# Two of four small tiled matmul groups moved to places where the TensorE tile shape changes anyway

## The chip, the cores and the metric

The kernel runs on one core of one Trainium2 (trn2) chip. The metric is the device time of one execution in microseconds (us). Times are medians of several executions. Each kernel also has one execution recorded by the hardware profiler; times inside it are counted from the first instruction. All runs told here are of the fast state, but for one single run (e8) whose state is unknown; the granted TensorE clock was 0.999 or 1.000 in all profiles.

## The reference, cut to what matters

Two attention blocks work on the same 2048 tokens (D = 1024, 32 heads of 32), and a gate mixes them. The change concerns block A, a linear attention:

```python
pq, pk = phi(q), phi(k)
kv  = einsum("bhsd,bhse->bhde", pk, v)      # one 32x32 matrix per head
num = einsum("bhqd,bhde->bhqe", pq, kv)
o   = num / (einsum("bhqd,bhd->bhq", pq, z)[..., None] + 1e-6)
a   = o.reshape(B, S, D) @ wo
...
return g * a + (1 - g) * b
```

The kernel never forms `num`. It multiplies each head's 32x32 `kv` into the 32 rows of `wo` that belong to the head, which gives a new weight "W2", and later applies W2 to the normalized `pq`. Making W2 is 64 small matmuls (32 rows, 32 columns of the array, 512 columns streamed), in four groups of 16, called events.

## The kernel before: the parts that matter

The kernel has eight banks of PSUM, the memory in which its matmuls accumulate. Four belong to `ps_pj`, the projection banks, a ring of buffers that every large matmul group uses. Four belong to `ps_1`, which exists only in the first stages; the score tile `s2b` and the output tile `po` of the next stage take over its banks.

```python
for g in range(2):                                    # KV, 128x64 tiles
    kvp = ps_1.tile([P, 4, 64], F32, name="kv_ps", tag="p1")
    for c in range(4):
        for kt in range(KT):
            for j in range(2): ...                    # 64 matmuls of 64 columns
    nc.vector.tensor_copy(out=KVT[:, 4 * g:4 * g + 4, :], in_=kvp[:])
# [...]
def w2_event(g, half):                                # 16 matmuls, 32x32 tiles
    def go():
        w2p = [ps_1.tile([P, 512], F32, name="w2_ps", tag="p1") for _ in range(4)]
        for j in range(4):
            for r in range(4):
                rs = slice(32 * r, 32 * r + 32)
                nc.tensor.matmul(w2p[r][32 * j:32 * j + 32, :],
                                 lhsT=KVT[rs, 4 * g + j, (r % 2) * 32:(r % 2) * 32 + 32],
                                 rhs=WoA[half][rs, 4 * g + j, :], start=True, stop=True)
        for r in range(4):
            (nc.scalar.copy if r % 2 else nc.vector.tensor_copy)(
                out=WoA[half][:, 4 * g + r, :], in_=w2p[r][:])
    return go
# [...]
units = [u for t in range(4) for u in v_units(t)]     # V projection, 128x128 tiles
interleave(units, [(8 + 12 * (2 * g + half), w2_event(g, half)) for g in range(2) for half in range(2)])
for t in range(12):                                   # the query stage
    for u in v_units(4 + t): u()
    for u in qa_units(t, bank1, qa_finish): u()       # qa_finish: phi, then normalize on VectorE
# [...]
nc.vector.memset(po[:], 1.0)                          # po lies in banks that ps_1 gave back
# [...] then the quads: K and Q of block B in 64x64 tiles, four slots of 8 steps each
```

TensorE's order is the program's, and VectorE's is too inside the first and the later stages. The memset of `po` stands between these, and the scheduler of the kernel language puts it into VectorE's order where its model thinks fit. A quad fills four banks, in four slots (the prediction counts them from one: its "second slot" is slot 1). Slots 0 and 1 each add the first half of the sums of two banks, a tiny read ("seen") separates them from slots 2 and 3, and then ScalarE and VectorE copy the banks out as `kt` and `qz`.

The softmax here doesn't subtract the row's maximum and nothing guards it: scores larger than these inputs give would overflow.

## Time and profile before

| what | before |
|---|---|
| time, median of 3 | 473.01 us (472.91 to 473.46) |
| span in the profile | 471.7 us |
| TensorE busy | 467.6 us, 99% |
| chain of waits: TensorE's share | 98% |
| four W2 events | about 1.9 us (worked out below; the printed chain counts 4 x 0.36 = 1.4 us) |

In the views PE stands for TensorE's matmuls, PEld for its weight loads, DVE for VectorE, ACT for ScalarE, POOL for GpSimd and SP for SyncE, which issues the DMA transfers; a "q" behind a name is that engine's sequencer. The page of the kernel before: the span, the busy line (engine, busy us, share of the span, instructions) and the chain that ended last, by engine.

```profile
span 471.7 us, 13176 instructions
...
PE 467.6 (99%) x5765; PEld 251.1 (53%) x5765; DVE 278.4 (59%) x602; ACT 168.7 (36%) x272; POOL 15.3 (3%) x30
...
PE 98%; DMA 1%; DVE 0%; issue 0%; DVEq 0%
```

TensorE is almost never idle and holds 98% of the chain, so in the main only TensorE's own time, or a wait of TensorE, can change the total. Here is TensorE in the V stage (timeline view; columns: start us, us, engine and line, operation, out<-in, shapes, count; in brackets the idle time before it and what ended it, "issue" where the profile shows nothing that did).

```profile
116.27 2.21 PE L240 MATMUL kv_ps<-G,WvA 128*64 128x64 bf16 x128
118.41 1.90 PE L295 MATMUL p_ps<-WvB,xT 128*128 128x512 bf16 x8
120.24 0.43 PE L283 MATMUL w_ps<-WoA,KVT 32*32 32x512 bf16 x16
120.61 2.76 PE L295 MATMUL p_ps<-WvB,xT 128*128 128x512 bf16 x12
123.30 0.43 PE L283 MATMUL w_ps<-WoA,KVT 32*32 32x512 bf16 x16
123.67 2.76 PE L295 MATMUL p_ps<-WvB,xT 128*128 128x512 bf16 x12
```

Two V groups of 12 matmuls start at 120.61 and 123.67, so 3.06 us pass for 12 full matmuls and one event. Full matmuls start 216 ns apart; 12 of them are 2.59 us, and the event costs 0.47 us. Its `busy` of 0.43 us is no measure of that, because matmuls overlap at both ends. The starts of single matmuls show what the 0.47 us is made of:

| step between two starts | ns |
|---|---|
| full matmul to full matmul | 216 |
| last full matmul to first W2 matmul | 309 |
| first to last of the 16 W2 matmuls | 50 |
| last W2 matmul to first full matmul | 318 |
| first full matmul to the second | 226 |

So 309 + 50 + 318 + 226 - 2 x 216 = 471 ns. A W2 matmul streams as many columns as a full one (216 ns), so 93 and 102 ns of the two changes of the tile shape are no streaming. The Trainium skill says in "TensorEngine Tiling (Array Packing)", Key Properties, that changing the tiling mode drains the TensorE. The trace fits that and gives the price, but it does not show that the drain is all of it: between full matmuls a weight load starts 214 ns before its own matmul, at the two changes only 1 and 4 ns before (the two loads take 88 and 96 ns), so a weight load that is no longer hidden is a rival. The 50 ns for 16 starts agree too with "TensorE: Matmul & The Clock Gate", Part 3, which counts about 4 ns per further tile; here it is 3.3.

Last, the border between the query stage (128x128 tiles) and the quads (64x64 tiles), in the timeline of the kernel before.

```profile
217.09 1.92 PE L388 MATMUL q_ps<-xT,WkB 64*64 64x512 bf16 x32
...
218.29 0.69 DVE L157 SCALAR_TENSOR_TENSOR tmp<-p_ps,e 128x512 bf16<-128x512 f32 x1
218.63 0.11 PEld L388 LDWEIGHTS <-WqB 64*64 64x64 bf16 x2
218.84 2.11 PE L388 MATMUL q_ps<-xT,WqB 64*64 64x512 bf16 x32
...
219.04 1.43 PEld L388 LDWEIGHTS <-WqB 64*64 64x64 bf16 x30 [0.30 <-issue]
```

Slot 1 of the first quad (the group of 218.84) fills two banks; one is the bank of the last query group, which VectorE's last phi (218.29 + 0.69 = 218.98) still reads. The slot's matmuls other than the first cannot start before 219.04, 0.19 us late: that is the break between the two weight-load lines. The view names no releaser for it ("issue"); in e6 below, where the same wait is longer, it names this phi. The engine's matmul lines show no gap here, because a matmul is recorded for longer (376 to 400 ns) than the 216 ns to the next one in its tile.

### The profile page before, as it was taken

The numbers are of one execution on the slowest core, as the hardware profiler recorded it, in microseconds if no ns is written. First come the engines' busy times: TensorE is split into PE (matmuls) and PEld (weight loads), VectorE is DVE, ScalarE is ACT, GpSimd is POOL, SyncE is SP. The second block draws the span as 40 slices with busy tenths as digits, with TensorE's granted clock in tenths as the row PEclk, the third lists the DMA queues.
The fourth block names the chain that finished last, engine by engine and source line by source line (L and its number), as shares of the span: only waits on it lengthen the run. The fifth ranks groups of instructions, "written<-read, shape, count | busy, mean of one in ns | idle before, by whom it ended". The sixth has DMA issues, their size and how long they took to land.

```text
span 471.7 us, 13176 instructions
## 1 busy us (share of the span) xinstructions
PE 467.6 (99%) x5765; PEld 251.1 (53%) x5765; DVE 278.4 (59%) x602; ACT 168.7 (36%) x272; POOL 15.3 (3%) x30
## 2 busy tenths in 40 slices
PE   8999999999999999999999999999999999999997
PEld 5444444445444444445677777777764444444444
DVE  0586689990329999999567676767670049800000
ACT  1343321112443333333555555555551134221121
POOL 3300000500000000000000000000000000000000
PEclk9999999999999999999999999999999999999999
DMA  8999970000643233627326364632563913221101
GB/s 220 193 246 374 348 248 0 0 1 1 213 134 108 92 142 128 156 96 248 103 56 100 71 91 96 91 93 63 93 173 67 227 64 79 69 54 45 35 33 46
DMA packets 98732, 55.40 MB, mean 117 GB/s; under 512 B 70130, under 2 KB 90610, under 8 KB 98674
## 3 DMA queue, kind: packets, MB, share of 16 engines
q1 hardware_dynamic: 93378, 49.87, 41.1%
q10 hardware_dynamic: 5296, 4.69, 2.9%
q8 instruction: 45, 0.74, 0.7%
q14 instruction: 13, 0.11, 0.1%
HBM read 26.10 MB, written 15.86 MB: 89 GB/s over the span
## 4 chain that ended last, share of the span: by engine, by line
PE 98%; DMA 1%; DVE 0%; issue 0%; DVEq 0%
PE q_ps L388 27%; PE d_ps L592 12%; PE p_ps L295 12%; PE pk_ps L169 12%; PE g_ps L220 12%; PE e_ps L592 12%; PE p_ps L331 9%; PE po L467 2%; PE s2b L445 2%; DMA xT<-in_A_x_dram 1%; PE kv_ps L240 0%; PE w_ps L283 0%; DVE osb L599 0%; DVEq L599 0%
## 5 line engine op out<-in xcount | busy, mean ns | idle before, releaser
L388 PE MATMUL q_ps<-xT,WqB 64*64 64x512 bf16 x1024 | 69.7, 377 | 0.0
L388 PE MATMUL q_ps<-xT,WkB 64*64 64x512 bf16 x1024 | 69.0, 376 | 0.0
L156 DVE TENSOR_SCALAR e<-e 128x512 f32<-128x512 f32 x64 | 27.1, 423 | 64.0 <-ACT e L155 64.0
L295 PE MATMUL p_ps<-WvB,xT 128*128 128x512 bf16 x256 | 57.9, 379 | 0.0
L169 PE MATMUL pk_ps<-WkA,xT 128*128 128x512 bf16 x256 | 55.7, 380 | 0.4 <-DMA xT<-in_A_x_dram 0.4
L220 PE MATMUL g_ps<-pk,xrow 128*128 128x512 bf16 x256 | 55.4, 379 | 0.0
L450 ACT ACTIVATE PT<-s2b 128x928 bf16<-128x928 f32 (+4 forms) x40 | 34.1, 854 | 45.5 <-PE s2b L445 45.5
L452 DVE TENSOR_TENSOR PT<-PT,mask 128x928 bf16<-128x928 bf16 (+4 forms) x40 | 23.6, 589 | 36.2 <-ACT PT L450 36.2
L331 PE MATMUL p_ps<-WqA,xT 128*128 128x512 bf16 x192 | 43.4, 379 | 0.0
L592 PEld LDWEIGHTS <-pqT 128*128 128x128 bf16 x272 | 26.0, 98 | 29.8 <-issue 0.4
L592 PEld LDWEIGHTS <-OBT 128*128 128x128 bf16 x272 | 26.0, 98 | 29.4
L169 PEld LDWEIGHTS <-xT 128*128 128x128 bf16 x256 | 25.0, 98 | 30.9 <-DMA xT<-in_A_x_dram 0.7
L220 PEld LDWEIGHTS <-xrow 128*128 128x128 bf16 x256 | 25.0, 98 | 30.2
L295 PEld LDWEIGHTS <-xT 128*128 128x128 bf16 x256 | 24.6, 98 | 30.0 <-issue 0.9
L388 PEld LDWEIGHTS <-WkB 64*64 64x64 bf16 x1024 | 34.0, 107 | 11.6 <-issue 0.4
L388 PEld LDWEIGHTS <-WqB 64*64 64x64 bf16 x1024 | 32.5, 107 | 11.1 <-issue 1.0
L599 DVE TENSOR_SCALAR osb<-e_ps,omg 128x128 bf16<-128x128 f32 x1 | 0.4, 351 | 57.6 <-PE e_ps L592 57.6
L155 ACT ACTIVATE e<-pk_ps 128x512 f32<-128x512 f32 x32 | 18.9, 597 | 40.5 <-PE pk_ps L169 36.3
L300 ACT CAST tmp<-p_ps 128x512 bf16<-128x512 f32 x32 | 18.7, 589 | 37.1 <-PE p_ps L295 32.3
L592 PE MATMUL d_ps<-WoA,pqT 128*128 128x512 bf16 (+1 forms) x136 | 30.9, 370 | 0.0
L331 PEld LDWEIGHTS <-xT 128*128 128x128 bf16 x192 | 18.8, 98 | 22.6
L592 PE MATMUL d_ps<-WoB,OBT 128*128 128x512 bf16 (+1 forms) x136 | 30.8, 370 | 0.0
(63 smaller groups left out, 530.3 us busy)
## 6 DMA issues: line engine op xcount, KB each, us to landing
vd<-tmp SPq DMA_DIRECT2D x16, 264.0 KB
xrow<-in_A_x_dram SPq DMA_DIRECT2D x4, 1024.0 KB
out_dram<-osb ACTq DMA_DIRECT2D x31, 128.0 KB
pqd<-tmp SPq DMA_DIRECT2D x12, 256.0 KB
WvA<-in_A_wqkv_dram SPq DMA_DIRECT2D x2, 1024.0 KB
WoA<-in_A_wo_dram SPq DMA_DIRECT2D x2, 1024.0 KB
WvB<-in_B_wqkv_dram SPq DMA_DIRECT2D x2, 1024.0 KB
WqA<-in_A_wqkv_dram SPq DMA_DIRECT2D x2, 1024.0 KB
```

The costliest lines, as they stand in the source:

```text
L155: nc.scalar.activation(out=e[:], in_=pj[:], func=ACT.Exp)
L156: nc.vector.tensor_scalar(out=e[:], in0=e[:], scalar1=1.0, scalar2=1e-6, op0=ALU.min, op1=ALU.add)
L169: nc.tensor.matmul(pj[:], lhsT=xT[:, kt, t * P:(t + 1) * P], rhs=WkA[half][:, kt, :], start=(kt == 0), stop=(kt == KT - 1))
L220: nc.tensor.matmul(pj[:], lhsT=xrow[:, t, kt * P:(kt + 1) * P], rhs=pk[:, t, half * 512:(half + 1) * 512], start=(t == 0), stop=(t == NB - 1))
L295: nc.tensor.matmul(st["pj"][:], lhsT=xT[:, kt, t * P:(t + 1) * P], rhs=WvB[half][:, kt, :], start=(kt == 0), stop=(kt == KT - 1))
L300: nc.scalar.copy(out=v[:, half * 16:(half + 1) * 16, 0:Dh], in_=st["pj"][:].rearrange("p (h e) -> p h e", h=16))
L331: nc.tensor.matmul(st["pj"][:], lhsT=xT[:, kt, t * P:(t + 1) * P], rhs=WqA[half][:, kt, :], start=(kt == 0), stop=(kt == KT - 1))
L388: nc.tensor.matmul(banks[o][64 * j:64 * j + 64, :], lhsT=lhsT(r, kt, j), rhs=rhs(r, kt), start=first and kt == 0, stop=kt == KT - 1, skip_ ...
L445: nc.tensor.matmul(s2b[64 * par:64 * par + 64, pair, :, o:o + w], lhsT=kts[c][r, par, k0:k0 + 64], rhs=qz[r, :, par, q0 % 512:q0 % 512 + w ...
L450: nc.scalar.activation(out=pt[:, :, 0:W_], in_=s2b[:].rearrange("p a b s -> p (a b) s")[:, :, 0:W_], func=ACT.Exp, scale=SCALE)
L452: nc.vector.tensor_tensor(out=pt[:, :, 0:W_], in0=pt[:, :, 0:W_], in1=mask[:, None, base:base + W_].broadcast_to([P, 4, W_]), op=ALU.mult)
L592: nc.tensor.matmul(st["ps"][:, 0:n], lhsT=lhsT, rhs=W[c0 // 512][:, c, c0 % 512:c0 % 512 + n], start=(side == 0 and c == 0), stop=(side == ...
```

## The change

Events should stand where the tile shape changes anyway. The first goes right behind KV (128x64 tiles to 128x128), the last to the end of the query stage (128x128 to 64x64). KV moves to the projection banks, so that the early event finds its own four free. At the end of the query stage VectorE is busy, so ScalarE alone empties the last event's banks. The whole diff:

```diff
--- before.py
+++ after.py
@@ -232,14 +232,14 @@
 
 
             for g in range(2):
-                kvp = ps_1.tile([P, 4, 64], F32, name="kv_ps", tag="p1")
+                kvp = ps_pj.tile([P, 512], F32, name="kv_ps", tag="pj")[:, 0:256].rearrange("p (c d) -> p c d", c=4)
                 for c in range(4):
                     for kt in range(KT):
                         for j in range(2):
                             cols = slice(c * P + 64 * j, c * P + 64 * j + 64)
                             nc.tensor.matmul(kvp[64 * j:64 * j + 64, c, :], lhsT=WvA[g][:, kt, cols],
                                              rhs=G[g][:, kt, cols], start=(kt == 0), stop=(kt == KT - 1))
-                nc.vector.tensor_copy(out=KVT[:, 4 * g:4 * g + 4, :], in_=kvp[:])
+                nc.vector.tensor_copy(out=KVT[:, 4 * g:4 * g + 4, :], in_=kvp)
             WkB = load_w("WkB", B_wqkv, D, "wb")
 
 
@@ -274,7 +274,7 @@
 
 
 
-            def w2_event(g, half):
+            def w2_event(g, half, engines=(nc.vector.tensor_copy, nc.scalar.copy)):
                 def go():
                     w2p = [ps_1.tile([P, 512], F32, name="w2_ps", tag="p1") for _ in range(4)]
                     for j in range(4):
@@ -284,8 +284,7 @@
                                              lhsT=KVT[rs, 4 * g + j, (r % 2) * 32:(r % 2) * 32 + 32],
                                              rhs=WoA[half][rs, 4 * g + j, :], start=True, stop=True)
                     for r in range(4):
-                        (nc.scalar.copy if r % 2 else nc.vector.tensor_copy)(
-                            out=WoA[half][:, 4 * g + r, :], in_=w2p[r][:])
+                        engines[r % len(engines)](out=WoA[half][:, 4 * g + r, :], in_=w2p[r][:])
                 return go
 
             def v_units(t):
@@ -345,12 +344,14 @@
                     nc.sync.dma_start(out=pqd[t * P:(t + 1) * P, :], in_=pn)
 
             units = [u for t in range(4) for u in v_units(t)]
-            interleave(units, [(8 + 12 * (2 * g + half), w2_event(g, half)) for g in range(2) for half in range(2)])
+            w2_event(0, 0)()
+            interleave(units, [(20, w2_event(0, 1)), (40, w2_event(1, 0))])
             for t in range(12):
                 for u in v_units(4 + t):
                     u()
                 for u in qa_units(t, bank1, qa_finish):
                     u()
+            w2_event(1, 1, (nc.scalar.copy,))()
             WqB = load_w("WqB", B_wqkv, 0, "wc")
```

## The prediction

> **What bounds the kernel now.** TensorE does: busy 467.6 of 471.7 us (the page's busy table), and the chain of waits is TensorE for 98% of the span. Only TensorE time on that chain counts. The four W2 events are 1.4 us of it, so all that can be won is small.
>
> **What one event costs** (single instructions of the trace, 119.9 to 123.9 us). A full 128x128 matmul starts 216 ns after the one before it. Where the array goes from 128x128 to 32x32 tiles the step is 309 ns. The 16 W2 matmuls then start within 50 ns, the first full matmul follows 318 ns after the last of them, and the next one is 10 ns late. So one event between full matmuls costs 309+50+318+10-216 = 471 ns; four of them 1.88 us. About 95 to 105 ns of each switch is not streaming. The Trainium skill, TensorEngine Tiling (Array Packing), Key Properties, says that changing the tiling mode drains the TensorE; the trace agrees: from the last KV matmul (128x64 tiles, 16 ns apart) to the first full one takes 128 ns, and from full tiles to the 64x64 tiles of the next stage 309 ns.
>
> **What the change does.** No matmul and no byte is added or removed. Each of the two moved events comes to stand where the tile shape changes anyway, so one switch less is paid: KV to W2 (est. 128 ns), 50, W2 to full 318 replaces KV to full 128. The event costs 368 ns instead of 471: 103 ns saved. At the end, full to W2 309, 50, W2 to 64x64 318 replaces 309: again 368, 103 ns saved. Together about 0.2 us, all on the critical path. KV in the projection banks only frees the four W2 banks for the early event; KV's first copy on VectorE ends at 117.93 us and the KV matmuls at 118.3, so the event should not wait. WoA landed at 57 us.
>
> **A second gain.** In the first quad of the 64x64 stage the second slot's WqB matmul waits from 218.85 to 219.04 us for the bank that VectorE's last phi frees at 218.996 us; three of the four tiles lose 0.19 us. In the new order VectorE's work moves forward with the query matmuls by 0.57 us (0.10+0.47), the stage itself by only 0.21, so this wait should vanish: 0.19 us.
>
> **What could be given back.** ScalarE copies four W2 banks (0.54 us each, back to back) from about 217.2 to 219.4, then does the two "seen" reads that the third slot waits for (its start about 220.2): about 0.4 us of slack, no stall. The memset of po (0.91 us, VectorE, now at 131.6 us in an idle moment) has to wait for the last event's banks, so it moves into or behind the last normalization, shortly before the first qz evictions. VectorE's normalization should end near 223.1, with the memset 224.1; qz becomes ready about 224.0 to 224.15. Roughly zero slack. If the memset is placed before the normalization instead, VectorE waits for ScalarE and TensorE stalls up to 0.9 us at the second quad's second slot (there is a 0.3 us wait already, at 226.07).
>
> **Prediction.** 473.01 - 0.10 - 0.10 - 0.19 = 472.6 us; 80% range 472.2 to 473.3. Faster by over 2%: 0.002; within 2%: 0.996; slower: 0.002.
>
> **Right if the trace shows:** no wait at KV to W2 and a step near 128 ns; two W2 events left between full matmuls at 471 ns; the 64x64 stage starting about 0.2 us earlier; no 0.19 us wait in its second slot; ScalarE's "seen" reads before the third slot.
>
> **Wrong if:** a switch costs differently by tile shape, the scheduler places the memset badly, or ScalarE's copies hold up the seen reads.

## The result, and the profile after

The changed kernel took 472.58 us (472.48 to 472.95, 5 runs) against 473.22 us (472.91 to 473.46, 5 runs) of the kernel before. The ratio is 0.999, with a 95% interval of 0.9976 to 1.0003; it holds 1, so by whole times alone the gain is not shown. A ratio here is the mean time of one kernel's runs over that of the other's of the same rounds, so it is not quite the ratio of the medians. The forecast was 472.6 us.

A part of this difference has nothing to do with the change, so the two profiles have to be compared piece by piece. The last KV matmul starts at 118.284 us before and at 118.105 after, although both programs are the same up to there but for the banks of KV, and KV itself takes 2.019 us from its first start to its last in both: the first stage waits for the transfer of x, and over 14 profiles this start lay between 117.80 and 118.37 us, once at 120.54. From here on I therefore count from the last KV matmul ("late query matmuls" are those of the last four row blocks, which run in 64x64 tiles behind the quads' K and Q):

| us | before | before, profiled again (e8) | after | after again (e11) |
|---|---|---|---|---|
| last KV matmul to first V matmul | 0.128 | 0.128 | 0.494 | 0.493 |
| last KV matmul to first quad matmul | 98.810 | 98.810 | 98.598 | 98.597 |
| first quad matmul to first score matmul | 9.625 | 9.624 | 9.420 | 9.420 |
| from there to the late query matmuls | 116.075 | 115.847 | 115.863 | 115.852 |
| last KV matmul to the end | 353.378 | 353.152 | 352.744 | 352.740 |

Apart from stray pauses (under e8), two executions of one program agree to about 0.01 us in these rows. That is far finer than the whole time, which scatters by some tenths. The page after has these lines in the same places.

```profile
span 470.8 us, 13145 instructions
...
PE 465.1 (99%) x5735; PEld 249.2 (53%) x5765; DVE 277.2 (59%) x600; ACT 169.7 (36%) x274; POOL 15.3 (3%) x30
...
PE 85%; SPq 11%; DMA 2%; DVE 1%; issue 1%; ACT 0%; DVEq 0%
```

Neither the lower busy time nor the chain's 85% means that TensorE works less. The profile holds 5735 matmuls instead of 5765, while both kernels have 5765 weight loads, so some records are missing. At one such hole, the second V matmul after the first event, the printed chain breaks ("issue"), and on the page it runs off to the load of `WvB`, whose two transfers had landed by 61.4 and 64.4 us, over 54 us earlier.

TensorE after the change, in the timeline:

```profile
116.09 2.21 PE L240 MATMUL kv_ps<-G,WvA 128*64 128x64 bf16 x128
118.23 0.43 PE L283 MATMUL w_ps<-WoA,KVT 32*32 32x512 bf16 x16
118.60 4.49 PE L294 MATMUL p_ps<-WvB,xT 128*128 128x512 bf16 x19
123.02 0.43 PE L283 MATMUL w_ps<-WoA,KVT 32*32 32x512 bf16 x16
123.39 4.49 PE L294 MATMUL p_ps<-WvB,xT 128*128 128x512 bf16 x19
```

The event follows KV at once (126 ns after the last KV matmul, as KV to V took 128 ns before), and the first V matmul comes 318 ns after the last of W2. At the border to the quads the steps are 310, 50 and 315 ns where 309 ns stood before. Two events are left between full matmuls, with 20 of these in between (one record is missing in each of the two groups of 19). And the border to the quads:

```profile
216.34 0.43 PE L283 MATMUL w_ps<-WoA,KVT 32*32 32x512 bf16 x16
...
216.70 1.92 PE L389 MATMUL q_ps<-xT,WkB 64*64 64x512 bf16 x32
216.94 2.05 ACT L287 CAST WoA<-w_ps 128x512 bf16<-128x512 f32 x4
...
217.53 0.69 DVE L157 SCALAR_TENSOR_TENSOR tmp<-p_ps,e 128x512 bf16<-128x512 f32 x1
...
218.24 1.63 PEld L389 LDWEIGHTS <-WqB 64*64 64x64 bf16 x32
...
218.45 1.90 PE L389 MATMUL q_ps<-xT,WqB 64*64 64x512 bf16 x32
218.83 0.41 ACT L401 COPY seen<-q_ps 128x1 f32<-128x1 f32 x2
...
220.18 1.90 PE L389 MATMUL q_ps<-xT,WkB 64*64 64x512 bf16 x32
...
220.95 0.91 DVE L373 MEMSET po<- 128x1024 f32 x1 [0.21 <-ACT seen L401]
...
223.96 1.41 DVE L428 TENSOR_SCALAR qz<-q_ps,qsel 128x512 bf16<-128x512 f32 x2
...
225.48 0.84 PE L389 MATMUL q_ps<-xT,WqB 64*64 64x512 bf16 x12
```

Three things are to be seen. VectorE's last phi is over at 218.23 and slot 1 starts at 218.45 with all its tiles: its 32 weight loads are one unbroken group now. ScalarE's four copies (216.94, 2.05 us) and the "seen" reads (218.83) are over at 219.24, 0.9 us before slot 2 (220.18) needs them. The memset of `po` sits inside VectorE's last normalization (220.95, after 0.21 us of idling), and the qz copies follow the normalization without a gap at 223.96. Slot 1 of the second quad waits for them about 0.3 us (225.48), as it did before.

### The profile page after: what moved, and what is told of

It reads as the page before. It is cut to its first block, busy times and chain, and to the rows that moved or that the text cites. A ratio compares the mean times of both kernels' runs of the same rounds, so it can differ in the third digit from the quotient of the medians.

```text
span 470.8 us, 13145 instructions
## 1 busy us (share of the span) xinstructions
PE 465.1 (99%) x5735; PEld 249.2 (53%) x5765; DVE 277.2 (59%) x600; ACT 169.7 (36%) x274; POOL 15.3 (3%) x30
## 4 chain that ended last, share of the span: by engine, by line
PE 85%; SPq 11%; DMA 2%; DVE 1%; issue 1%; ACT 0%; DVEq 0%
PE q_ps L389 27%; PE d_ps L593 12%; PE e_ps L593 11%; PE g_ps L220 11%; PE p_ps L294 11%; PE p_ps L330 8%; SPq L115 4%; SPq L81 4%; DMA WvB<-in_B_wqkv_dram 2%; PE po L468 2%; PE s2b L446 2%; SPq L94 1%; SPq L119 1%; SPq L98 1%; SPq L89 1%
## 5 line engine op out<-in xcount | busy, mean ns | idle before, releaser
L389 PEld LDWEIGHTS <-WkB 64*64 64x64 bf16 x1024 | 32.6, 107 | 12.4 <-DMA vd<-tmp 0.2
```

Of the source, the lines that this page charges most:

```text
L389: nc.tensor.matmul(banks[o][64 * j:64 * j + 64, :], lhsT=lhsT(r, kt, j), rhs=rhs(r, kt), start=first and kt == 0, stop=kt == KT - 1, skip_ ...
```

## The experiments

All twelve gave correct results. "Span" is the time from the last KV matmul to the end in the profile; the kernel before has 353.15 (e8), the changed kernel 352.74. The last column has the kernel before.

| run | median us (runs) | ratio to before, 95% interval | span us | before, median us |
|---|---|---|---|---|
| e1 first event only | 472.97 (5) | 0.9994, 0.9982 to 1.0006 | 353.06 | 473.19 |
| e2 last event only | 472.78 (5) | 0.9992, 0.998 to 1.0004 | 352.91 | 473.19 |
| e3 KV in the old banks | 473.48 (6) | 1.0012, 0.9999 to 1.0026 | 353.32 | 473.19 |
| e4 both engines empty the last event | 473.92 (5) | 1.0016, 1.0003 to 1.0029 | 354.04 | 473.19 |
| e8 before again | 472.97 (1) | none | 353.15 | 472.88 |
| e5 memset twice | 473.47 (4) | 1.0011, 0.9997 to 1.0024 | 353.70 | 472.88 |
| e6 last event 16 matmuls earlier | 473.36 (5) | 1.0006, 0.9992 to 1.0019 | 353.62 | 472.88 |
| e7 an event in front of the output stage | 472.55 (5) | 0.9993, 0.998 to 1.0005 | 352.69 | 472.88 |
| e9 as e6, memset later | 472.78 (4) | 0.9994, 0.998 to 1.0007 | 353.04 | 472.94 |
| e10 the change, memset later | 472.48 (4) | 0.999, 0.9977 to 1.0004 | 352.75 | 472.94 |
| e11 the change again | 472.91 (5) | 0.9998, 0.9985 to 1.0012 | 352.74 | 472.94 |
| e12 e7 again | 472.50 (5) | 0.9988, 0.9975 to 1.0 | 352.69 | 472.94 |

My theory has two parts: a switch of the tile shape saved per moved event (0.10 us each), and a bank wait that vanishes because VectorE's work moves forward more than the quads do (0.19 us). The rivals put the gain on one of the events alone, on the banks, or on ScalarE's doing the copies.

### e1 and e2: each event alone

```diff
 # e1, against the changed kernel
-interleave(units, [(20, w2_event(0, 1)), (40, w2_event(1, 0))])
+interleave(units, [(20, w2_event(0, 1)), (32, w2_event(1, 0)), (44, w2_event(1, 1))])
-w2_event(1, 1, (nc.scalar.copy,))()
 # e2, against the changed kernel; KV goes back to ps_1
-w2_event(0, 0)()
-interleave(units, [(20, w2_event(0, 1)), (40, w2_event(1, 0))])
+interleave(units, [(8, w2_event(0, 0)), (20, w2_event(0, 1)), (40, w2_event(1, 0))])
```

> Only the first W2 event is moved (right behind KV, KV in the projection banks); the other three stay between full matmuls at 20, 32 and 44. Theory (a saved switch of the tiling, and, apart from it, a saved bank wait that belongs to the last event): from the last KV matmul to the first V matmul 0.49 us instead of 0.13, one event of 0.47 us less in the V stage, so the 64x64 stage starts 0.10 us earlier counted from the last KV matmul; the 0.19 us wait at the second slot of the first quad stays. About 0.10 us below before. Rival (both gains come from the early event): the wait goes too, 0.30 us below before.

> Only the last event is moved to the end of the query stage (ScalarE alone empties it); KV keeps its old banks and the first three events stay at 8, 20 and 40. Theory: the 64x64 stage starts 0.10 us earlier counted from the last KV matmul and the 0.19 us wait at the second slot of the first quad is gone; 0.30 us below before, 0.10 above the whole change. Rival (gain needs the early event): the wait stays, 0.10 us below before.

| us | before | e1 | e2 | both |
|---|---|---|---|---|
| last KV matmul to first quad matmul | 98.810 | 98.703 | 98.703 | 98.598 |
| first quad matmul to first score matmul | 9.624 | 9.625 | 9.420 | 9.420 |

Each event saves 0.106 us in front of the quads, and the savings add up. The bank wait stays in e1 (slot 1 of the first quad is late from 218.64 to 218.84) and is gone in e2. So the second gain belongs to the last event alone. The times, 0.22 and 0.41 us below before, have the right order, but their intervals hold 1. In the span e1 gains 0.096 us and e2 0.242 us, which is 0.07 us less than the change's 0.408 us together: 0.06 us of that is a pause of e2 among the late query matmuls (15.383 us from there to the output stage, 15.32 to 15.33 in e1 and in both kernels), whose cause I did not trace.

### e3: KV's banks

```diff
-kvp = ps_pj.tile([P, 512], F32, name="kv_ps", tag="pj")[:, 0:256].rearrange("p (c d) -> p c d", c=4)
+kvp = ps_1.tile([P, 4, 64], F32, name="kv_ps", tag="p1")
```

> The whole change, but KV back in the banks of the W2 events. Theory: the fourth matmul of the early event needs the bank from which VectorE copies KV's second half until about 118.77 us, so TensorE waits from 118.24 to about 118.81 us: 0.55 us lost, and the time ends near 473.1, above before's by what is not covered. Rival (the banks do not matter, the copy is done in time): no wait, time as of the whole change, 472.6.

The timeline of e3 behind KV (this profile began 2.3 us late, in the first stage):

```profile
120.66 0.39 PE L283 MATMUL w_ps<-WoA,KVT 32*32 32x512 bf16 x3
...
120.78 0.42 DVE L242 CAST KVT<-kv_ps 128x256 bf16<-128x256 f32 x1 [0.59 <-PE kv_ps L240]
121.25 0.43 PE L283 MATMUL w_ps<-WoA,KVT 32*32 32x512 bf16 x13 [0.20 <-DVE KVT L242]
...
121.61 0.82 PE L294 MATMUL p_ps<-WvB,xT 128*128 128x512 bf16 x3
```

Three W2 matmuls run, then TensorE waits for VectorE's copy of KV (to 121.20) and goes on at 121.25. From the last KV matmul to V it takes 1.077 us instead of 0.494, so 0.58 us are lost, 0.55 expected. That is more than the whole change gains: in the span e3 is 0.17 us slower than the kernel before. No run moves KV alone, but e1 leaves nothing for it to have saved: its 0.107 us in front of the quads is the one switch. Without the move the early event costs more than it brings.

### e4, e5, e10: how much room VectorE has behind the query stage

```diff
 # e4
-w2_event(1, 1, (nc.scalar.copy,))()
+w2_event(1, 1)()
 # e5
 nc.vector.memset(po[:], 1.0)
+nc.vector.memset(po[:], 1.0)
 # e10: the memset not here, but in the quads' list of events
-nc.vector.memset(po[:], 1.0)
+events.insert(0, (32, lambda: nc.vector.memset(po[:], 1.0)))
```

> The whole change, but the last event's four banks are shared by VectorE and ScalarE as the others are. VectorE's order is the program's, so its two copies (1.3 us) and then the memset of po come behind the last normalization and before the first qz evictions. Theory (VectorE has no slack there): qz starts about 1.25 us later and the second slot of the second quad with it: 1.2 us above the whole change, 473.8. Rival (VectorE's lag is absorbed by the buffers behind it): within 0.2 us of the whole change.

> The whole change with the memset of po done twice on VectorE (0.91 us more in front of the first qz evictions). Theory (no slack left): the qz evictions start 0.9 us later and so does the second slot of the second quad; 0.9 us above the whole change, 473.5. Rival (VectorE still has room): within 0.2 us of the whole change.

> The whole change with the memset of po behind the first qz evictions, out of VectorE's last normalization. Theory (the memset uses up VectorE's slack but no more than that): qz starts at the same time, because it waits for TensorE's last matmul of the quad; span from the last KV matmul 352.74 us as in the whole change, within 0.05. Rival (the memset holds qz up): the 0.33 us wait at the second slot of the second quad shrinks.

The timeline of e4, VectorE's copies of the last event, the memset, the qz copies and slot 1 of the second quad:

```profile
222.79 1.28 DVE L287 CAST WoA<-w_ps 128x512 bf16<-128x512 f32 x2
...
224.43 0.91 DVE L373 MEMSET po<- 128x1024 f32 x1 [0.36 <-DVE WoA L287]
...
225.25 1.32 DVE L428 TENSOR_SCALAR qz<-q_ps,qsel 128x512 bf16<-128x512 f32 x2
...
226.70 0.84 PE L389 MATMUL q_ps<-xT,WqB 64*64 64x512 bf16 x12 [1.24 <-ACT qz L426]
```

VectorE's copies come behind its normalization and push the memset and qz back. TensorE idles 1.24 us before slot 1 of the second quad (226.70), until ScalarE's qz copy, which takes turns with VectorE's on the same banks, is done. From the first quad matmul to the first score matmul e4 takes 10.71 us instead of 9.42, 1.29 us more; in time it is the only run whose interval lies wholly above 1. e5 takes 10.25, 0.83 us more. A further 0.13 us of e5 is a stray pause near 244 us, of the kind described under e8.

In e10 VectorE has the memset behind qz:

```profile
221.47 1.29 DVE L320 TENSOR_TENSOR tmp<-tmp,den 128x512 bf16<-128x512 bf16 x2
...
223.77 1.41 DVE L427 TENSOR_SCALAR qz<-q_ps,qsel 128x512 bf16<-128x512 f32 x2 [1.01 <-PE q_ps L388]
...
225.39 0.91 DVE L511 MEMSET po<- 128x1024 f32 x1 [0.21 <-issue]
```

Now the normalization ends at 222.76 at the latest, VectorE idles 1.01 us before qz, for TensorE, and nothing gets faster (9.421 us). In the changed kernel VectorE idles 0.019 us between the normalization and qz. So it uses up VectorE's room of 1.0 us to the last 0.02 us, and no more. The rival of e4, that buffers absorb the lag, falls.

### e6 and e9: the same event 16 matmuls earlier

```diff
-for u in qa_units(t, bank1, qa_finish):
+for i, u in enumerate(qa_units(t, bank1, qa_finish)):
+    if t == 11 and i == 0:
+        w2_event(1, 1, (nc.scalar.copy,))()
     u()
-w2_event(1, 1, (nc.scalar.copy,))()
 # e9: in addition the memset as in e10
```

> The whole change, but the last event (ScalarE alone) stands 16 full matmuls before the end of the query stage instead of at the border to the 64x64 tiles. Theory: it costs 0.47 us there instead of 0.37, and since the delay now comes before VectorE's last phi, that phi no longer gets ahead of TensorE: the wait of 0.1 to 0.2 us at the second slot of the first quad comes back. 0.2 to 0.3 us above the whole change. Rival (the gain comes from ScalarE alone emptying the banks, or from the event's lateness): as fast as the whole change.

In e6 the stage before the quads took 98.703 us, 0.105 us more than with the event at the border, as expected. But slot 1 of the first quad waited 0.76 us, not 0.1 to 0.2: my expectation missed. The timeline shows why.

```profile
216.24 0.91 DVE L374 MEMSET po<- 128x1024 f32 x1 [0.21 <-ACT e L155]
...
218.57 0.69 DVE L157 SCALAR_TENSOR_TENSOR tmp<-p_ps,e 128x512 bf16<-128x512 f32 x1
...
219.31 1.06 PE L390 MATMUL q_ps<-xT,WqB 64*64 64x512 bf16 x16 [0.39 <-DVE tmp L157]
```

The scheduler had put the memset of `po` in front of VectorE's last two phis, so the last phi ended 0.57 us later than in the kernel before, counted from the first quad matmul (2.46 us behind it instead of 1.89). That is the 0.76 us less the old 0.19. The experiment had changed two things. e9 takes the memset out of the way.

> As e6 (last event 16 full matmuls before the end), but the memset of po, which in e6 the scheduler put in front of VectorE's last phi, is placed behind the first qz evictions, so that only the event's place differs. Theory: what e6 waited more than 0.2 us was the memset; here the second slot of the first quad waits 0.15 to 0.2 us, as in the kernel before, and the event costs 0.10 us more than at the border: 0.3 us above the whole change, the span from the last KV matmul about 353.04 us. Rival (the wait is of another making): the 0.76 us wait of e6 stays, or there is none.

```profile
217.97 0.69 DVE L157 SCALAR_TENSOR_TENSOR tmp<-p_ps,e 128x512 bf16<-128x512 f32 x1
...
218.53 1.68 PE L389 MATMUL q_ps<-xT,WqB 64*64 64x512 bf16 x25
...
218.72 1.22 PEld L389 LDWEIGHTS <-WqB 64*64 64x64 bf16 x27 [0.30 <-issue]
```

The wait is 0.19 us again (218.53 to 218.72), as in the kernel before, and the span is 353.038 us, with 353.04 expected; e10, which has the memset in the same place and the event at the border, has 352.748. So both gains of the last event come from its place, after VectorE's last input and at the border; ScalarE's doing the copies brings nothing by itself; it only avoids what e4 lost. And where the memset falls is worth 0.58 us (353.62 against 353.04), more than the whole change.

### e8 and e11: the two kernels again

> The kernel before, unchanged, profiled once more. Its first trace has a TensorE pause of 0.21 us near 274.7 us that no semaphore explains and that neither the changed kernel nor the first four experiments show. If the pause belongs to that one execution, it is gone here, and the span counted from the last KV matmul is 353.17 us instead of 353.38. If it belongs to the program before, it is here again, and 0.2 us of the measured gain came from nothing that the change intended. The 0.19 us bank wait at the second slot of the first quad should be there either way.

> The changed kernel once more, beside e12 on the same chip. Theory: span from the last KV matmul 352.74 us, 0.41 us less than the kernel before without its stray pause; time 0.4 us below before of the same rounds. Rival (the first comparison, 0.64 us, was right): 0.6 us below.

The first profile of the kernel before has this line at 274.69 us, a weight load that comes 0.32 us after the engine's last one, with no releaser but "issue".

```profile
274.69 0.35 PEld L388 LDWEIGHTS <-WqB 64*64 64x64 bf16 x10 [0.32 <-issue]
```

In e8, the same program, it is gone, and the span is 353.152 us. So it belonged to that execution. Pauses like it (0.13 us in e5 at 244 us) come and go; what makes them I do not know. The real gain of the change is 353.152 - 352.744 = 0.41 us, and e11 repeats the 352.74. The whole times bracket it without settling it: in means, 0.52 us in the first comparison (473.19 against 472.67), 0.19 us in e11's (473.05 against 472.86). The rival of e11, a gain of 0.6, falls.

### e7 and e12: one event more to a border

```diff
-interleave(units, [(20, w2_event(0, 1)), (40, w2_event(1, 0))])
+interleave(units, [(20, w2_event(0, 1))])
-w2_event(1, 1, (nc.scalar.copy,))()
+w2_event(1, 0, (nc.scalar.copy,))()
 # at the start of the output stage, in its four banks ps_3, on both engines
+w2_event(1, 1, pool=ps_3, tag="p3")()
 # [...] w2_event takes pool and tag as arguments, ps_1 and "p1" by default
```

> The idea carried on: event (1,0) takes the place at the end of the query stage, and event (1,1) goes to the border between the 64x64 tiles and the output matmuls, in the banks of the output stage, shared by VectorE and ScalarE; one event is left between full matmuls. Theory: another 0.10 us saved, 0.10 us below the whole change, provided the copies are done before the output matmuls need WoA's second half at about 2.6 us into the stage. Rival (the output stage waits for the copies or for the banks): slower than the whole change by what it waits, up to 1 us.

> e7 once more (event (1,0) at the end of the query stage, event (1,1) in front of the output matmuls), beside the changed kernel on the same chip. Theory: without e7's stray pause the span from the last KV matmul is 0.10 us shorter than that of the whole change, 352.64 us; the time 0.1 us lower, which is less than the runs scatter. Rival (the 0.06 us of e7's profile is all): 352.69.

The timeline of e7 at the border between the late query matmuls and the output stage:

```profile
357.14 0.43 PE L283 MATMUL w_ps<-WoA,KVT 32*32 32x512 bf16 x16
...
357.51 1.90 PE L593 MATMUL d_ps<-WoA,pqT 128*128 128x512 bf16 x7
357.67 1.29 DVE L287 CAST WoA<-w_ps 128x512 bf16<-128x512 f32 x2 [3.44 <-PE w_ps L283]
...
358.21 1.09 ACT L287 CAST WoA<-w_ps 128x512 bf16<-128x512 f32 x2
...
359.25 1.89 PE L593 MATMUL e_ps<-WoA,pqT 128*128 128x512 bf16 x8
```

The event costs 0.366 us there (15.688 us from the late query matmuls to the output stage, 15.322 before, in e8), and the stage before the quads is 0.472 us shorter; this is the 0.10 us expected. VectorE is idle at this place, so here two engines do no harm (one alone was not tried): the copies end at 359.3 us, before the matmuls that read them at about 360. But 0.06 us are given back near 327.8 us, where one slot of a quad starts late for a ScalarE copy, in both profiles of this program. The span is 352.686 us both times, so the theory's 352.64 misses and the rival's 352.69 holds. I traced that wait to VectorE's copies of the group before, which start 0.07 us later in relation to the first quad matmul, and no further; its cause stays open. e12 is the fastest of the kernels by its span, 0.05 to 0.06 us below the change, and by its mean in that call (472.50 against 472.86), but a tenth is less than the runs scatter.

## Why the prediction was right

- **The size.** 472.6 us was forecast and 472.58 measured, but this agreement to 0.02 us is partly luck: the time scatters by some tenths, and the forecast counted from 473.01 us, while the five runs of the comparison gave 473.22 for the kernel before, so that 0.64 us came off in medians where 0.39 was forecast. The span is the sharper test: a gain of 0.39 us was forecast and 0.41 measured.
- **One switch less per moved event.** Forecast 103 ns each, measured 106 (e1, e2). KV to W2 was estimated at 128 ns from KV to V, and took 126. That estimate could hold because the price hardly depends on the shapes here: the switches after matmuls of 512 columns, in both kernels and in e7, left 90 to 102 ns beside the streaming.
- **The bank wait.** Forecast 0.19 us, measured 0.204 (9.624 to 9.420), and by e1, e2 and e9 it belongs to the last event's place.
- **No wait for KV's copy.** Right, and e3 shows that the banks are what makes it right.
- **ScalarE's copies in time for the "seen" reads.** Right; the room was 0.9 us and not 0.4. Counted from the last KV matmul, the copies ended 0.23 us earlier and the third slot began 0.16 us later than I had put them, and the reads overlap the copies by about 0.1 us.
- **"Roughly zero slack" for the memset.** Right to 0.02 us, and e4, e5 and e10 show both sides of it. I had thought that the memset would go "into or behind the last normalization"; it went into it.
- What I named as the main risk, the place of the memset, was real: in e6 it cost 0.58 us.

## What to carry to other kernels

On an engine that is hardly ever idle, count the changes of the tile shape as well as the matmuls: each cost about 0.1 us here, and a group of small tiles placed where the shape changes anyway saved one. Before putting work at such a border, work out what the other engines do at that moment; a second copying engine cost 1.3 us in one place (e4) and did no harm in another (e7). Where gains are tenths of a microsecond, measure from a marker inside the profile behind the noisy part, and profile the kernel before twice.

## What the Trainium skill lacked or had wrong

- "TensorEngine Tiling (Array Packing)", Key Properties, says that a change of the tiling mode drains the TensorE, but gives no price. Here 90 to 102 ns per switch behind a matmul of 512 columns, between 128x128, 64x64 and 32x32 tiles (how much of it is the drain stays open); 16 matmuls of 32x32 tiles between full ones cost 471 ns, of which 216 are streaming.
- The same page, PSUM Bottleneck, says to use both ScalarE and VectorE for PSUM evacuation. Both did it without harm where both had room (e7). Where VectorE had a backlog, sharing the four banks made the kernel 1.3 us slower (e4).
- No page that I read tells of stray TensorE pauses without a semaphore (0.13 and 0.21 us here), nor that two profiles of one program otherwise agree to about 0.01 us behind a marker (98.810 and 98.810, 98.598 and 98.597 us).
